# Two mixture-of-experts blocks on one core: weight conversions of the second block spread over both layers, and both entries rearranged

## The chip, the cores and the metric

One core of a Trainium2 chip runs the whole kernel. The metric is the device time of one launch in microseconds (us), the median of the runs shown.

The engines are called as in the profile: PE is TensorE (matmuls; PEld its weight loads), DVE is VectorE, ACT is ScalarE, POOL is GpSimd, SP is SyncE, which here only issues DMAs. Each engine works through its own instructions in order, and waits for others by semaphores.

## The reference

An attention-like layer (8 x 8 heads, 576 rows, no softmax, a decaying causal mask) makes 4608 rows of 512 numbers. Two mixture-of-experts (MoE) blocks with 8 experts follow.

```python
def _moe_ref(x, w_skip, w_gate, w1, w2):          # first block
    do_compute = x @ w_skip > 0
    xc = x[do_compute]
    e_idx = np.argmax(xc @ w_gate, axis=1)
    gate_w = softmax(xc @ w_gate)[chosen]
    for e in range(E):
        h = np.maximum(xc[mask] @ w1[e], 0.0)
        y[mask] = gate_w[mask, None] * (h @ w2[e])
    out[do_compute] = xc + y

def _moe2_ref(x, w_gate, w1, w2):                 # second block
    cap = N // E                                  # 576
    logits = x @ w_gate
    for idx in np.argsort(-logits.flatten()):     # best pair first
        tok, e = idx // E, idx % E
        if assigned[tok] >= 0 or counts[e] >= cap: continue
        assigned[tok] = e; counts[e] += 1
    for e in range(E):
        h = np.maximum(x[mask] @ w1[e], 0.0)      # 512 -> 1024
        out[mask] = h @ w2[e]                     # 1024 -> 512
```

## The kernel before

**Stages.** Attention runs first, up to about 176 us. The first MoE block runs its eight experts (e = 0 to 7) from there to about 480, the second block its eight (i = 0 to 7, in the order in which experts fill up) from there to the end. An expert is a gather of its rows by POOL, a turn of each tile of 128 rows (four transposes on PE, line 641; ACT writes the high half xTH, line 642; DVE the low half xTL, line 179), layer 1 and layer 2.

**Numbers in two halves.** Matmuls of both layers take fp32r operands, and each product is made of three matmuls: high by high, high by low, low by high. So weights too are split: a quarter of w1 or w2 (512 KB) is loaded into one of five `wraw` buffers (`w_load`, line 234), ACT copies it to the high half (`w_split`, line 245: w1H, w2H), and DVE subtracts to get the low half (`w_rest`: w1L, w2L). `halves(kind)` is a list of five jobs that do this for four quarters, the low half of one beside the high half of the next. In the second block, `w2`'s raw quarters stay in their buffers until the tail has read them.

**Layer 1** (`layer1`, `layer1_f`, line 660) goes over eight f of 128 hidden units, in two segments of columns in the second block, (0, 288) and (288, 576), with 12 matmuls each into one of three PSUM buffers. ACT writes hH (line 669), DVE hL (line 188). The last 64 columns go to hT. **Layer 2** has a tail of 64 rows (`layer2_half`, line 714, from hT and raw w2), then four tiles of 128 rows (`layer2`, line 691) with 24 matmuls of 512 columns each. The order of segments and f in a block is such that each w1 quarter serves two consecutive f.

**The first block's hand-written order.** `slot_a()` takes the next of `jobs` between pieces of a layer. The entry (from line 1047) makes three turns with warm-up matmuls between them (`warm`, line 224: 128 columns of ones), and steps the generator `gate_weights()` beside them: an Exp, three parts of gate weights multiplied into MV, and 36 small matmuls `gp` (line 832). In layer 1 of expert 0, the jobs are the loads of the next expert's w1, issued by ACT, and the last gate step. In layer 2, `gate_spread` (line 752) broadcasts the second block's gate weights by SP into the buffers that MV and OHlo leave, for the dot products `gate_dots` (line 758).

**The second block's routing chain.** `phase(i)` finds expert i and its list: five rounds of M (DVE), `cnt` (PE), `part` (DVE), `sum` (PE), `fl` (DVE), `nfl` (PE), `nf` (DVE); then `eix`, the expert's number (DVE); then `pfx`, slots, OHh, MV, OHl (DVE), `idp` and `idq` (PE, lines 1273 and 1282) and `ids2`, the list (DVE); then `cc`, `ccb`, `cct`, and the next phase's Lm, vq, c, mx, OH. `load_b(i)` reads `eix` into a register and makes the loads of this expert's weights.

**The planner.** In the second block PE calls `tick(cols)` within the layers; it advances a clock by cols/2400 and steps each task that is due. A task is a generator that yields the time to its next step; a step is due its yield after the later of its own due time and the clock less 0.4. There are three tasks: the chain of phases, `weights_b(i)` and `rows_b(i)`. In `weights_b(i)`, first the jobs of `halves("w2")` come, 2.3 apart, in layer 1; when expert i+1 is known, its first w1 quarter is loaded; after the tail the three others, then `halves("w1")`, 2.3 apart, then four w2 loads. `rows_b(i)` issues five gathers when the list is there, and five turns, 1.3 apart.

**The second entry** (from line 1372). `late()` runs the last layers of the first block with phase 0; when expert 0 is known, SP loads its two first w1 quarters. When the list is there, five gathers and the conversion of these quarters come, 30 warm-up matmuls, and then turns and steps of the chain (`go`) alternate, with the other loads (two w1 and two w2 quarters by ACT, behind the second turn).

Of the kernel before, what the change touches and what calls it, by code (L numbers as in the profile page):

```python
# [23 lines left out]
P = 128  # L24
# [138 lines left out]
def block_kernel(ctx, tc, q_c, k_c, k_r, v_r, wg, wg2, w1a, w2a, w2t, w1b, w2b, cst, dtab, out, dbg=None):  # L163
# [794 lines left out]
    eix = rt("eix", [P, E], I32)  # L958
    lo0 = rt("lo0", [P, 1])
# [91 lines left out]
    for n, j in enumerate(t0):  # L1051
        next(gws)
        warm(ps1, "l1", 16 if n == 0 else 4)
        j()
    next(gws)
# [34 lines left out]
    for e in range(LATE):  # L1090
        jobs = halves("w2") if e else []
        ga, (la1, la2) = gathers_a(e + 1), loads_a(e + 1)
        if e == 0:
            sta = state()
            jobs += [la1[0], la1[1], lambda: next(gws, None), la1[2], la1[3]]
        else:
            jobs = jobs[0:2] + [ga[0]] + jobs[2:4] + [ga[1]] + jobs[4:5] + [ga[2]] + la1
# [62 lines left out]
    def phase(i):  # L1160
# [124 lines left out]
        ts(iv, p[:, 5:10], -1.0, ALU.add)  # L1285
        stt(ids2[:, i, :], p[:, 0:5], 64.0, iv, ALU.mult, ALU.add)
# [67 lines left out]
    def load_b(i, eng=nc.sync):  # L1354
        r = eng.value_load(eix[0:1, i:i + 1], min_val=0, max_val=E - 1)
        return loads_dyn(r, w1b, w2b, eng=eng)
# [4 lines left out]
    def late():  # L1361
        yield 1.0
        gate_h(1, 0, hh, 7)
        for d in gate_slots(1, L2[:, NT:NC, :]):
            yield d
        for d in last_claims():
            yield d
        for d in phases():
            if not lb and 0 in know:
                lb.extend(load_b(0))  # L1370
                for j in lb[0][0:2]:
                    j()
            yield d

    lb = []
# [5 lines left out]
    while 0 not in listed:  # L1381
        next(gen)
    sp = halves("w1", swap=True)
    for j in gathers_b(0) + sp[0:2]:
        j()
    t0 = turns(("b", 0), T2, (2, 3))
    warm(ps1, "l1", 30)
    go = lambda: next(gen)
    la = load_b(0, nc.scalar)
    for j in [go, go, t0[0], go, t0[1], go] + la[0][2:4] + [t0[2], go, t0[3], la[1][0], la[1][1]] + sp[2:5] + lb[1][2:4]:  # L1390
        j()
# [19 lines left out]

    def weights_b(i):
        for j in halves("w2", swap=True):
            j()
            yield 2.3
# [5 lines left out]
        l1[0]()  # L1421
        while lay[0] < 2 * i + 1 or ("tail", i) not in done:
            yield 0
        for j in l1[1:]:
            j()
        for j in halves("w1", swap=True):
            j()
            yield 2.3
        for j in l2:
            j()  # L1430

    def rows_b(i):
# [7 lines left out]
        yield 3.5  # L1440
        while lay[0] < 2 * i + 1:
            yield 0
        for j in turns(("b", i + 1), T2):
            j()
            yield 1.3

    for i in range(E):
        mine = [task(weights_b(i)), task(rows_b(i))]
        ht = xp.tile([P, 8, 64], F32, name="hT", tag="junk", bufs=1)
        hh = layer1(("b", i), [(0, 288), (288, CAP2)], lambda: None, 1 if i else 2, tick, ht=ht)  # L1450
# [43 lines left out]
```

## Time and profile before

| | us |
|---|---|
| median of 3 runs | 983.54 (982.27 to 983.57) |
| the profiled execution, its own time | 981.48 |
| its span from the first to the last instruction | 979.6 |
| PE busy | 922.7 (94%) |
| DVE busy | 651.1 (66%) |
| ACT busy | 321.9 (33%) |
| POOL busy | 236.1 (24%) |
| mean granted TensorE clock | 0.981 of full |

All stretches and rows are in us from the start of the span of the profiled execution. A row of the timeline gives start, duration, engine, line and operation, the tile written and those read, and in brackets the idle time of its engine before it and what ended it. Durations of PE include the matmul's way through the array, so matmuls in a row overlap; PEclk is the granted clock, 1.00 for 2.4 GHz and 0.50 for 1.2 GHz. The stages can be found by time: first entry 176 to 192, experts of the first block to 480, second entry 480 to 495, blocks 0 to 7 of the second block from 495, 565.5, 626.3, 687.0, 747.6, 808.8, 868.4 and 922.4 on (block 0 lasts to 565.5).

### The profile page before, as it was taken

The page shows a single profiled execution, that of the slowest core. Times are in us where ns is not written, and L with a number is a line of the kernel's source. Part 1 is how long each engine was busy: PE and PEld are TensorE (multiplying, and loading weights), DVE is VectorE, ACT ScalarE, POOL GpSimd, SP SyncE. Part 2 cuts the span into 40 slices and gives each one's busy share as a digit, 9 for nine tenths or more (in the row PEclk, how much of TensorE's full clock was granted, in tenths as well). Part 3 has the DMA queues.
Part 4 walks back from the last instruction along what each step waited for, and adds up shares of the span by engine and source line. Part 5 has one row for each costly group of instructions (what it writes and reads, how often), then busy time and mean ns, then how long its engine had stood idle before and what let it go on. Part 6 is the DMA issues. An engine that isn't in the chain of part 4 may idle for free.

```text
span 979.6 us, 20718 instructions
## 1 busy us (share of the span) xinstructions
PE 922.7 (94%) x8322; PEld 774.5 (79%) x8322; DVE 651.1 (66%) x1676; ACT 321.9 (33%) x610; POOL 236.1 (24%) x208
## 2 busy tenths in 40 slices
PE   8999998599999999998789999999999999999997
PEld 7778876498888888886578697887978869787886
DVE  4566675449999999966686767667676676744230
ACT  1233333133434334351142233332433324333320
POOL 2322231203264334322200303103031030330101
PEclk9999999799999999999979999999999999999999
DMA  9999995355454455330242406125060240732301
GB/s 336 348 372 376 345 358 202 89 206 175 145 206 136 161 178 193 111 133 11 93 166 88 171 12 213 56 74 186 11 234 36 96 163 12 236 103 97 103 6 43
DMA packets 57684, 153.96 MB, mean 157 GB/s; under 512 B 8464, under 2 KB 9232, under 8 KB 57328
## 3 DMA queue, kind: packets, MB, share of 16 engines
q1 hardware_dynamic: 40608, 107.50, 31.4%
q0 software_dynamic: 10496, 30.93, 9.2%
q10 hardware_dynamic: 6480, 14.16, 3.9%
q8 instruction: 67, 1.10, 0.4%
q14 instruction: 33, 0.27, 0.1%
HBM read 127.43 MB, written 25.13 MB: 156 GB/s over the span
## 4 chain that ended last, share of the span: by engine, by line
PE 64%; DVE 23%; DMA 6%; issue 5%; ACT 1%; POOL 0%; SPq 0%; POOLq 0%; ACTq 0%; DVEq 0%
PE l1p L660 27%; PE l2p L691 19%; DVE junk L758 5%; PE l2p L714 3%; DVE w1L L179 3%; PE xTp L445 3%; DVE w2L L179 2%; PE sc L419 2%; DMA X<-xo 2%; DVE xTL L179 2%; PE trp L641 2%; PE xrp L473 1%; PE xTp L442 1%; DMA kT<-in_k_c_dram 1%; DMA qT<-in_q_c_dram 1%
## 5 line engine op out<-in xcount | busy, mean ns | idle before, releaser
L660 PE MATMUL l1p<-xTH,w1H 128*128 128x288 f32 (+1 forms) x768 | 243.2, 317 | 3.6 <-DVE hL L188 2.7
L660 PE MATMUL l1p<-xTL,w1H 128*128 128x288 f32 (+1 forms) x768 | 236.2, 308 | 2.8 <-DVE xTL L179 2.7
L660 PE MATMUL l1p<-xTH,w1L 128*128 128x288 f32 (+1 forms) x768 | 235.3, 306 | 0.0
L691 PE MATMUL l2p<-w2H,hH 128*128 128x512 f32 (+1 forms) x448 | 186.2, 416 | 0.0
L691 PE MATMUL l2p<-w2H,hL 128*128 128x512 f32 (+1 forms) x448 | 176.1, 393 | 0.0
L691 PE MATMUL l2p<-w2L,hH 128*128 128x512 f32 (+1 forms) x448 | 175.3, 391 | 0.0
L660 PEld LDWEIGHTS l1p<-xTH,w1H 128*128 128x128 f32 x768 | 146.5, 191 | 7.9 <-DVE hL L188 5.4
L660 PEld LDWEIGHTS l1p<-xTL,w1H 128*128 128x128 f32 x768 | 146.5, 191 | 3.9 <-DVE xTL L179 3.6
L660 PEld LDWEIGHTS l1p<-xTH,w1L 128*128 128x128 f32 x768 | 146.4, 191 | 0.0
L188 DVE SCALAR_TENSOR_TENSOR hL<-l1p,hH 128x288 fp32r<-128x288 f32 (+1 forms) x192 | 85.7, 453 | 87.2 <-ACT hH L669 85.5
L669 ACT ACTIVATE hH<-l1p 128x288 fp32r<-128x288 f32 (+1 forms) x192 | 78.5, 410 | 179.3 <-PE l1p L660 175.0
L720 POOL DMA_INDIRECT out_dram<-y,ids x40 | 43.3, 1084 | 378.5 <-DVE y L179 218.3
L691 PEld LDWEIGHTS l2p<-w2H,hH 128*128 128x128 f32 (+1 forms) x448 | 82.9, 185 | 23.9 <-issue 8.3
L758 DVE SCALAR_TENSOR_TENSOR junk<-x,wgb 128x512 f32<-128x512 f32 (+1 forms) x144 | 99.0, 688 | 3.1
L691 PEld LDWEIGHTS l2p<-w2H,hL 128*128 128x128 f32 (+1 forms) x448 | 82.6, 184 | 20.7
L691 PEld LDWEIGHTS l2p<-w2L,hH 128*128 128x128 f32 (+1 forms) x448 | 83.1, 185 | 15.0
L621 POOL DMA_INDIRECT xg<-X,ids x64 | 79.3, 1238 | 57.3 <-issue 22.5
L642 ACT ACTIVATE xTH<-trp 128x512 fp32r<-128x512 f32 (+2 forms) x64 | 35.6, 558 | 119.0 <-PE trp L641 91.4
L245 ACT ACTIVATE w1H<-wraw 128x1024 fp32r<-128x1024 f32 x64 | 65.2, 1053 | 25.0 <-DMA wraw<-in_w1b_dram 20.6
L179 DVE TENSOR_TENSOR w1L<-wraw,w1H 128x1024 fp32r<-128x1024 f32 x60 | 71.3, 1219 | 2.5 <-ACT w1H L245 2.0
L245 ACT ACTIVATE w2H<-wraw 128x1024 fp32r<-128x1024 f32 x64 | 67.3, 1054 | 17.2 <-PE l2p L691 7.3
L179 DVE TENSOR_TENSOR w2L<-wraw,w2H 128x1024 fp32r<-128x1024 f32 x60 | 72.7, 1213 | 0.0
(257 smaller groups left out, 1137.5 us busy)
## 6 DMA issues: line engine op xcount, KB each, us to landing
wraw<-in_w2a_dram SPq DMA_DIRECT2D x31, 512.0 KB
wraw<-in_w1b_dram SPq DMA_DIRECT2D x30, 512.0 KB
wraw<-in_w2b_dram SPq DMA_DIRECT2D x30, 512.0 KB
wraw<-in_w1a_dram SPq DMA_DIRECT2D x28, 512.0 KB
kT<-in_k_c_dram SPq DMA_DIRECT2D x36, 256.0 KB
qT<-in_q_c_dram SPq DMA_DIRECT2D x36, 256.0 KB
vR<-in_v_r_dram SPq DMA_DIRECT2D x36, 256.0 KB
X<-xo ACTq DMA_DIRECT2D x36, 256.0 KB
```

The costliest lines, as they stand in the source:

```text
L179: V.tensor_tensor(o, x, y, op)
L188: V.scalar_tensor_tensor(o, x, sc, y, op0, op1)
L245: nc.scalar.activation(h, r, AF.Copy)
L445: nc.tensor.matmul(xTp[o, hh, x:x + P], lhsT=d["vs"][:, 2 * pr + hh, :], rhs=d["ret"][:, hh, pr, :], start=(c == 0), stop=True, skip_group ...
L621: nc.gpsimd.indirect_dma_start(out=t[0:n, :], out_offset=None, in_=X[:, :], in_offset=bass.IndirectOffsetOnAxis(ap=ids[0:n, :], axis=0))
L642: nc.scalar.activation(h[:, :, off:off + n], p[:, :, 0:n], AF.Copy)
L660: nc.tensor.matmul(o, lhsT=wx[:, c:c + P], rhs=xx[:, k, a:b], start=(n == 0), stop=(n == 11))
L669: nc.scalar.activation(hh[0][:, f, a:b], o, AF.Relu)
L691: nc.tensor.matmul(p[0:n, :], lhsT=x[:, f, off:off + n], rhs=y[:, c:c + 512], start=(f == 0 and j == 0), stop=(f == 7 and j == 2))
L714: nc.tensor.matmul(p[64 * h:64 * h + 64, :], lhsT=ht[:, g], rhs=w[g // 2][:, c:c + 512], start=(f == 0), stop=(f == 3), tile_position=(0, ...
L720: nc.gpsimd.indirect_dma_start(out=dst[:, :], out_offset=bass.IndirectOffsetOnAxis(ap=idx, axis=0), in_=src[0:n, :], in_offset=None)
L758: V.scalar_tensor_tensor(j[0:n], x2[0:n], 1.0, wgb[e // 4][0:n, e % 4], ALU.mult, ALU.mult, accum_out=dst[0:n, e:e + 1])
```

## The change

Five things are changed.

1. First entry: the steps of `gate_weights()` no longer stand between the turns. All five go into the jobs of layer 1 of expert 0, alternating with the loads of the next w1; the last one (the matmuls gp) comes after layer 1.
2. Second entry: the loads of the first two w1 quarters come after the list, not when the expert is known, and read the expert's number from a copy `eil`, made just before the list. Their conversions move behind the first steps of the chain, between the turns. There are 64 warm-up matmuls, not 30.
3. Layer 1's segments in the second block are (0, 256) and (256, 576).
4. `weights_b(i)`: of the next expert's w1, quarter 0 is converted in layer 1, quarter 1 in layer 2, quarters 2 and 3 at the beginning of the next layer 1 (`held`), ahead of the w2 quarters. The last w2 load moves there too.
5. `rows_b(i)`: 2.6 instead of 3.5 before the turns, which are 1.8 apart instead of 1.3.

```diff
     t0 = turns(0, T1, (2,))
     for n, j in enumerate(t0):
-        next(gws)
         warm(ps1, "l1", 16 if n == 0 else 4)
         j()
-    next(gws)
     for j in gathers_a(1):
         j()
...
-            jobs += [la1[0], la1[1], lambda: next(gws, None), la1[2], la1[3]]
+            jobs += [j for n in range(4) for j in (lambda: next(gws, None), la1[n])] + [lambda: next(gws, None)]
...
         ts(iv, p[:, 5:10], -1.0, ALU.add)
+        if i == 0:
+            V.tensor_copy(eil, eix[:, 0:1])
         stt(ids2[:, i, :], p[:, 0:5], 64.0, iv, ALU.mult, ALU.add)
...
     def load_b(i, eng=nc.sync):
-        r = eng.value_load(eix[0:1, i:i + 1], min_val=0, max_val=E - 1)
+        r = eng.value_load(eix[0:1, i:i + 1] if i else eil[0:1, 0:1], min_val=0, max_val=E - 1)
...
         for d in phases():
-            if not lb and 0 in know:
-                lb.extend(load_b(0))
-                for j in lb[0][0:2]:
-                    j()
             yield d
...
+    lb = load_b(0)
     sp = halves("w1", swap=True)
-    for j in gathers_b(0) + sp[0:2]:
+    for j in lb[0][0:2] + gathers_b(0):
         j()
     t0 = turns(("b", 0), T2, (2, 3))
-    warm(ps1, "l1", 30)
+    warm(ps1, "l1", 64)
     go = lambda: next(gen)
     la = load_b(0, nc.scalar)
-    for j in [go, go, t0[0], go, t0[1], go] + la[0][2:4] + [t0[2], go, t0[3], la[1][0], la[1][1]] + sp[2:5] + lb[1][2:4]:
+    for j in [go, go, sp[0], t0[0], sp[1], go, t0[1], go] + la[0][2:4] + [t0[2], go, t0[3], la[1][0], la[1][1]] + sp[2:5] + lb[1][2:4]:
         j()
...
     def weights_b(i):
+        if held:
+            for c in (2, 3):
+                w_split("w1", c, "later", swap=True)
+                yield 1.2
+                w_rest("w1", c)
+                if c == 2:
+                    held.pop()()
+                yield 1.2
         for j in halves("w2", swap=True):
             j()
             yield 2.3
...
         l1, l2 = load_b(i + 1)
         l1[0]()
+        yield 3.0
+        w_split("w1", 0, "later", swap=True)
+        yield 1.5
+        w_rest("w1", 0)
         while lay[0] < 2 * i + 1 or ("tail", i) not in done:
             yield 0
         for j in l1[1:]:
             j()
-        for j in halves("w1", swap=True):
+        yield 2.3
+        w_split("w1", 1, "later", swap=True)
+        yield 2.3
+        w_rest("w1", 1)
+        for j in l2[0:3]:
             j()
-            yield 2.3
-        for j in l2:
-            j()
+        held.append(l2[3])
...
-        yield 3.5
+        yield 2.6
...
         for j in turns(("b", i + 1), T2):
             j()
-            yield 1.3
+            yield 1.8
...
-        hh = layer1(("b", i), [(0, 288), (288, CAP2)], lambda: None, 1 if i else 2, tick, ht=ht)
+        hh = layer1(("b", i), [(0, 256), (256, CAP2)], lambda: None, 1 if i else 2, tick, ht=ht)
```

## Rows read from the trace of the kernel before

**Rows 1.** Page, busy us of each engine, share of the span, instructions.

```profile
PE 922.7 (94%) x8322; PEld 774.5 (79%) x8322; DVE 651.1 (66%) x1676; ACT 321.9 (33%) x610; POOL 236.1 (24%) x208
```

**Rows 2.** Stretches: us; busy PE, PEld, DVE, ACT, POOL; PEclk, DMA share, GB/s.

```profile
534.03:565.53 31.50, 29.25 (x174) 21.81 (x175) 20.03 (x60) 9.19 (x13) 10.29 (x9) 0.95 0.51 180
565.53:593.26 27.73, 27.73 (x242) 26.84 (x243) 19.09 (x62) 11.00 (x27) 1.31 (x1) 1.00 0.08 30
...
596.84:626.30 29.46, 27.60 (x175) 20.91 (x175) 19.64 (x58) 9.08 (x13) 10.17 (x9) 1.00 0.55 192
...
778.94:808.75 29.81, 27.59 (x176) 20.94 (x175) 19.55 (x58) 9.08 (x13) 10.00 (x9) 1.00 0.53 190
840.06:868.36 28.30, 27.58 (x174) 21.34 (x174) 18.42 (x62) 9.07 (x13) 10.49 (x9) 1.00 0.64 220
```

**Rows 3.** PE's waits, 500 to 880: us in total, times, longest.

```profile
PE trp L641 <- DVE xTL L179: 6.8, 10, 2.0
```

**Rows 4.** PE in order of time: start, us, what, [idle before <- releaser].

```profile
552.08 0.65 PE L641 MATMUL trp<-cs,xg 128*128 128x128 f32 x4 [2.04 <-DVE xTL L179]
...
597.58 0.87 PE L1273 MATMUL idp<-MV,OHl 128*128 128x160 bf16 x10
...
612.94 0.66 PE L641 MATMUL trp<-cs,xg 128*128 128x128 f32 x4 [1.30 <-DVE xTL L179]
```

**Rows 5.** DVE in order of time, block 1, end of layer 1 and layer 2.

```profile
592.35 0.45 DVE L188 SCALAR_TENSOR_TENSOR hL<-l1p,hH 128x288 fp32r<-128x288 f32 x1
...
595.14 0.89 DVE L179 TENSOR_TENSOR OHl<-hl,kq 128x640 bf16<-128x640 bf16 x2
...
602.64 2.36 DVE L179 TENSOR_TENSOR w1L<-wraw,w1H 128x1024 fp32r<-128x1024 f32 x2
...
612.20 0.68 DVE L179 TENSOR_TENSOR xTL<-trp,xTH 128x512 fp32r<-128x512 f32 x1
```

**Rows 6.** ACT in order of time, end of block 1's layer 1.

```profile
591.70 0.41 ACT L669 ACTIVATE hH<-l1p 128x288 fp32r<-128x288 f32 x1 [1.28 <-PE l1p L660]
```

**Rows 7.** SP's queue, block 1, and DMA in a stretch (columns as rows 2).

```profile
588.51 8.69 SPq L234 DMA_DIRECT2D wraw<-in_w1b_dram  x4
...
591.25:591.50 0.25, 0.25 (x5) 0.25 (x4) 0.21 (x2) 0.00 (x0) 0.00 (x0) 1.00 0.01 0
```

**Rows 8.** First entry: PE, then DVE, then ACT, in order of time.

```profile
189.55 0.43 PE L660 MATMUL l1p<-xTH,w1H 128*128 128x352 f32 x1 [0.82 <-ACT xTH L642]
192.33 0.66 PE L660 MATMUL l1p<-xTL,w1H 128*128 128x352 f32 x1 [2.35 <-DVE xTL L179]
...
191.72 0.55 DVE L179 TENSOR_TENSOR xTL<-trp,xTH 128x384 fp32r<-128x384 f32 x1
...
189.01 0.49 ACT L642 ACTIVATE xTH<-trp 128x384 fp32r<-128x384 f32 x1 [0.20 <-PE trp L641]
```

**Rows 9.** Stretches at half clock, columns as rows 2.

```profile
191.20:194.70 3.50, 2.37 (x8) 2.38 (x9) 1.88 (x6) 0.00 (x0) 0.00 (x0) 0.51 0.21 83
194.70:198.10 3.40, 3.40 (x14) 3.40 (x13) 0.53 (x1) 0.46 (x1) 0.00 (x0) 0.50 0.28 98
553.20:556.60 3.40, 3.40 (x20) 2.73 (x20) 1.43 (x4) 0.54 (x2) 0.00 (x0) 0.51 0.10 36
```

**Rows 10.** Second entry: SP, ACT, POOL, the chain, PE, in order of time.

```profile
476.12 1.01 SPq L234 DMA_DIRECT2D wraw<-in_w1b_dram  x2
...
479.28 1.06 ACT L245 ACTIVATE w1H<-wraw 128x1024 fp32r<-128x1024 f32 x1 [10.85 <-DMA wraw<-in_w1b_dram]
...
483.16 0.92 POOL L720 DMA_INDIRECT X<-x,ids  x1 [5.23 <-DVE pt L1276]
486.70 1.01 POOL L621 DMA_INDIRECT xg<-X,ids  x1 [2.62 <-DVE X L179]
...
493.59 5.79 DMA wraw<-in_w1b_dram
...
504.03 0.41 PE L1192 MATMUL cnt<-OH,M 128*128 128x32 bf16 x10 [0.96 <-DVE M L179]
```

More of the change, by code (lines that the diff above doesn't have):

```diff
@@ L958, in block_kernel @@
     eix = rt("eix", [P, E], I32)
+    eil = rt("eil", [P, 1], I32)
     lo0 = rt("lo0", [P, 1])
@@ L1368, in late @@
         for d in phases():
-            if not lb and 0 in know:
-                lb.extend(load_b(0))
-                for j in lb[0][0:2]:
-                    j()
             yield d
-    lb = []
     gen = late()
@@ L1410, in block_kernel @@
     done = set()
+    held = []
     def weights_b(i):
+        if held:
[6 more added lines that the diff above has]
+                yield 1.2
         for j in halves("w2", swap=True):
```

## The prediction

> **What bounds the kernel now.** I read the page's engine shares first: TensorE (PE) is busy for 94% of the span [rows 1]. What a change can win is therefore the time in which PE waits or runs at half clock, at about 57 us in all. Next came the busy times by stretch. A block of the second MoE is layer 1, a half-tile tail and layer 2. In layer 1 (565.53 to 593.26) PE is busy for all of 27.73 us; in layer 2 it is busy for 27.6 us, but the stretch lasts 29.46 in block 1, the same within 0.1 in blocks 2 and 3, 29.81 in block 4, 28.30 in block 5 and 31.50 in block 0 [rows 2]. So each of these blocks leaves 0.7 to 2.3 us idle, all in layer 2. The waits say who: transposes (line 641) wait for xTL, 6.8 us in ten waits, the longest 2.0 [rows 3, 4]. VectorE (DVE) explains why: from 602.64 on it takes four w1L subtractions of 1.18 us amid the routing steps, and the first xTL ran only at 612.20 [rows 5]. The PSUM buffer came free late, and the third turn waited 1.30 us [rows 4]. Of the two entries I read PE and what ends its waits. At the first, the second matmul waits 2.35 us for the last xTL [rows 8], and the clock then falls [rows 9]. At the second, the chain runs through gathers and weight loads [rows 10].
>
> **The change, part by part.**
>
> *First entry.* The four gate-weight steps leave the stretch before layer 1. Two of them stood between the three xTL on DVE. Without them the last xTL needs only its xTH, which ends at 189.01 + 0.49 = 189.50 [rows 8]; with about 0.5 for the subtraction, PE goes on at 190.03 instead of 192.33: **2.3 us**. The steps (DVE work and one Exp) run under the first layer, where DVE has only one hL per f; without that cover they would cost the 2.3 us again. The 36 gp matmuls stay one run on PE, now after layer 1; no change. Queues they pass: ScalarE's (ACT) loads for expert 1 go out one to four slots later, still before layer 1 ends, and are converted in layer 2; SP's two gate-weight broadcasts wait for gp, so they move from the middle of layer 1 to its end, ahead of SP's w2 loads, and are first read after layer 2's first tile. I take 0 for both, and 1 us as the bad end.
> The clock: PE was at half speed from 191.2 to 198.1 (mean 0.51, then 0.50) [rows 9], with 2.37 + 3.40 = 5.77 us busy; at full speed this is half, **2.9 us** less. Does it still fall? In layer 2 a wait of 1.30 us did not lower the clock (block 1, 29.46 less 27.60 is all idle), one of 2.04 did [rows 2, 4, 9]. What is left here is the 0.82 before 189.55 [rows 8], nearer to the first: I take 2.9, with 0 as the other end. Entry one: **5.2**, ends 1.3 and 5.2.
> Ahead of 189.55 PE has transposes, with only a few warm-up matmuls between them. If these do not hold the clock, it falls as before, which is rival 1. The Trainium skill ("TensorE: Matmul & The Clock Gate", Part 4) has this as a rule: a transpose does not count as PE activity in the way that a matmul does. By that rule entry one would give 2.3 and not 5.2; the rows of before do not show which.
>
> *Second entry.* The two first w1 loads leave 476.12 [rows 10] for the time after the list. Gain: the scatter before the last ran beside them, so the last one left only at 483.16, after 5.23 us idle on GpSimd (POOL), and the first gather, which reads what it wrote, stood 2.62 us idle behind it, until 486.70 [rows 10]. Without the loads that gather starts up to 2.6 us earlier; I take 1.6, near 485.1. Loss: the loads now run beside the gathers, and w1H of the first quarter, which ACT takes in order, stands ahead of the first xTH, the second ahead of the second xTH. A load beside one scatter was taken up 479.28 - 476.12 = 3.16 us after its issue [rows 10]; issued after the list, near 485.3, the quarters land near 489 and, beside the gathers, 491, so the second xTH ends near 493. Only then does ACT issue the last two w1 quarters, at 493.59 before. The chain goes on from there as it did: 5.79 us of load [rows 10], w1H, w1L, the last xTL, OH, M, and the counting matmuls, on which PE waits at 504.03 [rows 10]. The 256-column first segment (two turns) and the 64 warm-up matmuls help PE before that point only, and PE waits there anyway. I take **0**, with -2 (load and gather slow each other as the scatter was) and +2 (all of the gather's lead) as ends; the copy into eil is inside these.
>
> *Segments.* Columns per f stay 576. No matmul of 256 columns with fp32r operands is in the trace: if each took as long as one of 288, the 96 of a block would lose a ninth of at most 27.73/192 = 0.144 each, 1.5 us a block and 12 in all. Ten matmuls of 160 columns take 0.87 [rows 4], 0.087 each, so I see no floor there and take 0.
>
> *Blocks.* I worked out the planner's clock (each tick adds columns/2400; a step is due its yield after the later of its due time and the clock less 0.4). Layer 1 is 23.04, the tail 3.41, layer 2 20.48, and the routing chain keeps its place, one list per block at 28.37. In blocks 1 to 5, w1 quarters 2 and 3 go to 0.6 to 4.2, the w2 quarters from 0.7-10.1 to 5.8-15.0, quarter 0 of the next expert to 20.8 and 22.2, quarter 1 stays in layer 2; the turns run from 34.1 in steps of 1.9. Layer 1's DVE goes from 19.09 to about 22.5 of 27.73 us, ACT's from 11.0 to 14.2 [rows 2]: no PE wait from load alone, since one subtraction (1.18) in front of a routing step is what w2L already does there without a wait.
> The last w2 quarter, loaded only when quarter 2 of w1 is done (2.1), is converted at 12.8, ten us later; SP has nothing queued behind it.
> In layer 2 one of three early w1L remains and the two around the turns go: the first xTL moves up from 612.2 by about 3 us, and the waits of [rows 3] go: 1.86 in block 1, 1.76 and 1.78 in 2 and 3, 2.2 in 4, 0.7 in 5.
> **What is late next** is the early quarter. Its load is issued at 588.51, when the expert is known; its packets end by 591.25 [rows 7], so it can be taken up at about 592.0. ACT comes to it before that and is held; after 1.06 of w1H the hH due at 591.70 [rows 6] starts at 593.1, hL behind it on DVE at 593.5 instead of 592.35, and the work from there to the end of OHl, 3.7 us almost without a gap [rows 5], plus the new w1L of 1.18, ends at 598.3. PE wants OHl at 597.6 to 597.7 [rows 4]: a new wait of **0.6 us** in each of blocks 1 to 5. So they give 1.26, 1.16, 1.18, 1.61 and 0.10: 5.3. In block 0 the expert is known at 19.20 of the planner's clock, not 17.28: two us later, so the wait is 2.6, over the 2.04 that lowered the clock, and that cost 29.25 busy us against 27.60, 1.65 more [rows 2]. Block 0: 27.6 + 2.6 + 1.65 = 31.85, **-0.3**. Blocks: **5.0**. Ends: 0 (the load 0.8 later) and 12.2 (no new wait).
>
> *Sum.* 5.2 + 0 + 5.0 = 10.2. The profiled execution took 981.48, 1.9 more than its span; it becomes 971.3. The median of the runs, 983.54, is 2.06 above it: **973.3 us**.
>
> **Rivals.**
> 1. *The clock falls at the first entry all the same*, because what stands ahead of 189.55 is mostly transposes. The gain is 2.3 there, 7.3 in all: 976.2. For it: the clock fell there before; against it: the wait of 2.35 that went with that is gone [rows 8, 9].
> 2. *The waits only change place.* The new wait at the list's matmuls eats what the turns give back (blocks: 0), loads and gathers hinder each other (-2), and the clock falls (2.3): 983.2, no change. For it: DVE is packed in that stretch [rows 5].
> 3. *Slower: the early load holds ACT past the end of layer 1.* If it is taken up 1.5 us later than I put it, the list's matmuls wait 2.1 us in blocks 1 to 5 and 4.1 in block 0, and each such wait lowers the clock as the 2.04 did: 27.6 + 2.1 + 1.65 = 31.35 against 29.4, five times 1.9, and 33.35 against 31.5: 11.3 lost, less 5.2: 989.6. It decides at a wait between 1.30 and 2.04 us, that is, a load 0.7 to 1.4 later. Against it: nothing else loads then; the 512 KB ran alone. For it: other ACT work is behind it in order.
> 4. *The load lands before ACT asks*: no new wait, 12.2 + 5.2: 966.1.
>
> **How the numbers follow.** Forecast 0.58 (its own range 968 to 979, by the ends of entry two and of the blocks together); rival 1 0.14, rival 2 0.13, rival 3 with the 256-column floor 0.12, rival 4 0.03. Faster by over 0.2% (2 us, about what can be told from no change): 0.58 + 0.14 + 0.03 = 0.75; within: 0.13; slower: 0.12. The range 967 to 982 leaves out rival 4, rival 3 and the upper half of rival 2, a little under 0.2.
>
> **What would show it.** Right: PE's second layer-1 matmul right after the first at the first entry, with no half clock until layer 1 ends; no wait of transposes for xTL in blocks 0 to 5; a wait of about 0.6 before idp (2.6 in block 0), with DVE's hL held by ACT; the second entry's M at the same distance from the list. Wrong: waits before counting matmuls in layer 1, w1H waiting for its load over 2 us, a PEclk under 1.0 in layer 2 of blocks 1 to 5, or layer 1 longer than 27.8 us.

## The result, and the profile after

| | us |
|---|---|
| before, median of 8 runs beside it | 983.18 (979.95 to 988.38) |
| after, median of 8 runs | 972.08 (969.09 to 978.59) |
| ratio, 95% interval | 0.9904 (0.9874 to 0.9934) |
| after, the profiled execution and its span | 971.05 and 969.3 |

The ratio is estimated from all runs; it is not the quotient of the two medians, which would be 0.9887. Forecast were 973.3 for the median and 971.3 for the profiled execution. Both sums came out nearly right, but two of the terms were wrong by 4 to 5 us, in opposite directions. So the profile comes first, in the order of the prediction.

The busy row of the page, after:

```profile
PE 918.6 (95%) x8356; PEld 768.9 (79%) x8356; DVE 653.6 (67%) x1677; ACT 320.2 (33%) x610; POOL 232.6 (24%) x208
```

PE does the same work in a shorter span [rows 1]. Now the stretches that answer [rows 2] (columns as there): layer 2 of block 0, layer 1 and layer 2 of block 1.

```profile
533.54:562.72 29.18, 27.66 (x175) 20.73 (x174) 19.43 (x62) 6.11 (x10) 8.89 (x9) 1.00 0.48 177
562.86:590.38 27.52, 27.52 (x240) 26.55 (x239) 20.70 (x59) 13.79 (x30) 1.30 (x1) 1.00 0.13 49
594.00:621.56 27.56, 27.56 (x176) 20.91 (x175) 17.41 (x59) 6.11 (x10) 10.21 (x9) 1.00 0.53 187
```

Layer 2 of block 1 has no idle time left (27.56 of 27.56, against 27.60 of 29.46), and layer 1 carries the moved work without a wait, with DVE at 20.7 of 27.5 us. Block 0 keeps 1.5 us idle, but its clock no longer falls (1.00, against 0.95). PE's waits from 500 to 880, the answer to [rows 3]:

```profile
PE idp L1272 <- DVE OHl L179: 1.8, 3, 0.9
PE l1p L660 <- DVE xTL L179: 1.4, 1, 1.4
PE cnt L1191 <- DVE M L179: 0.9, 1, 0.9
PE trp L641 <- DMA xg<-X,ids: 0.4, 1, 0.4
```

The ten waits of transposes for xTL are gone. The new wait before idp that I expected in every block is there in blocks 0 and 3 only. The first entry, answering [rows 8 and 9]: PE in order of time, then two stretches.

```profile
190.39 0.42 PE L660 MATMUL l1p<-xTH,w1H 128*128 128x352 f32 x1 [0.58 <-ACT xTH L642]
190.98 0.43 PE L660 MATMUL l1p<-xTL,w1H 128*128 128x352 f32 x1 [0.17 <-DVE xTL L179]
```

```profile
190.39:194.00 3.61, 3.44 (x20) 3.20 (x21) 1.36 (x3) 0.91 (x2) 0.00 (x0) 1.00 0.04 15
194.00:198.00 4.00, 4.00 (x27) 4.00 (x26) 2.46 (x9) 0.93 (x2) 0.00 (x0) 1.00 0.43 140
```

The 2.35 us wait has become 0.17, and the clock stays full. From the first layer-1 matmul to the first of layer 2 it took 22.01 us before (189.55 to 211.56) and takes 17.11 now (190.39 to 207.50).

Where the 10.4 us between the two profiled executions lie, worked out from such boundaries of PE in both traces (plus is gained): attention's end -0.7; first entry with the first expert's layer 1 +4.8; the rest of the first block's experts **-2.6**; second entry, up to the tail of block 0, -1.0; tail and layer 2 of block 0 +2.2; blocks 1 to 5 +2.1, +2.1, +1.7, +2.0, +0.7; blocks 6 and 7 **-0.4 and -0.5**. Nothing that I costed can lengthen the three stretches in bold. The last chain pieces show where the two at the end come from: in each kernel, the 192 layer-1 matmuls and the last 72 layer-2 matmuls of the last block, as the chain has them (start, us, what). Before, then after:

```profile
922.38 25.43 PE l1p L660 x192
951.39 16.58 PE l2p L691 x72
```

```profile
911.60 25.28 PE l1p L660 x192
940.46 17.01 PE l2p L691 x72
```

No wait and no lower clock is in them: the same 72 matmuls take 0.43 us longer. The same in the group of layer-2 matmuls of the first block (line 691, high half of h by low half of w2; busy us, mean ns of one), before, then after:

```profile
L691 PE MATMUL l2p<-w2L,hH 128*128 128x512 f32 x384 | 150.3, 391 | 0.0
```

```profile
L691 PE MATMUL l2p<-w2L,hH 128*128 128x512 f32 x384 | 151.6, 395 | 0.0
```

So three questions were put to the chip: did the clock at the first entry hold because the wait is gone; what in the blocks' part won, and why did the new wait stay away; and what slowed layer 2.

### The profile page after: what moved, and what is told of

It is laid out like the page before. It is cut to its first block, busy times and chain, and to the rows that moved or that the text cites. A ratio compares the mean times of both kernels' runs of the same rounds, so it can differ in the third digit from the quotient of the medians.

```text
span 969.3 us, 20752 instructions
## 1 busy us (share of the span) xinstructions
PE 918.6 (95%) x8356; PEld 768.9 (79%) x8356; DVE 653.6 (67%) x1677; ACT 320.2 (33%) x610; POOL 232.6 (24%) x208
## 4 chain that ended last, share of the span: by engine, by line
PE 72%; DVE 15%; DMA 7%; issue 3%; ACT 1%; SPq 1%; POOL 1%; POOLq 0%; ACTq 0%; DVEq 0%
PE l1p L660 27%; PE l2p L691 26%; DVE junk L758 5%; PE xTp L445 3%; PE trp L641 3%; PE l2p L714 2%; PE sc L419 2%; DVE w2L L179 2%; DMA vR<-in_v_r_dram 2%; DMA xg<-X,ids 2%; PE xrp L473 1%; DVE xTL L179 1%; DMA kT<-in_k_c_dram 1%; DVE hL L188 1%; PE xTp L442 1%
## 5 line engine op out<-in xcount | busy, mean ns | idle before, releaser
L660 PE MATMUL l1p<-xTH,w1H 128*128 128x320 f32 (+2 forms) x768 | 241.4, 314 | 4.9 <-DVE hL L188 3.0
L660 PE MATMUL l1p<-xTL,w1H 128*128 128x320 f32 (+2 forms) x768 | 234.2, 305 | 2.9 <-DVE xTL L179 2.9
L660 PE MATMUL l1p<-xTH,w1L 128*128 128x320 f32 (+2 forms) x768 | 233.7, 304 | 0.0
L188 DVE SCALAR_TENSOR_TENSOR hL<-l1p,hH 128x256 fp32r<-128x256 f32 (+1 forms) x192 | 85.6, 453 | 80.6 <-ACT hH L669 77.1
L669 ACT ACTIVATE hH<-l1p 128x256 fp32r<-128x256 f32 (+1 forms) x192 | 78.3, 408 | 147.7 <-PE l1p L660 141.1
```

Of the source, the lines that this page charges most:

```text
L188: V.scalar_tensor_tensor(o, x, sc, y, op0, op1)
L660: nc.tensor.matmul(o, lhsT=wx[:, c:c + P], rhs=xx[:, k, a:b], start=(n == 0), stop=(n == 11))
L669: nc.scalar.activation(hh[0][:, f, a:b], o, AF.Relu)
```

## The experiments

Each kernel ran beside the kernel before on one chip. The ratios:

| kernel | median us | before beside it | ratio to before, 95% interval |
|---|---|---|---|
| first entry alone (e1_gate) | 979.04 | 982.20 | 0.9961 (0.9939 to 0.9984) |
| blocks alone (e2_blocks) | 972.93 | 982.20 | 0.9906 (0.9875 to 0.9938) |
| second entry alone (e3_entry) | 988.39 | 982.20 | 1.0050 (1.0031 to 1.0070) |
| segments alone (e4_segs) | 985.50 | 982.20 | 1.0017 (0.9995 to 1.0039) |
| unused 4-byte tile (g1_pad32) | 986.79 | 981.93 | 1.0048 (1.0027 to 1.0068) |
| unused 64-byte tile (g2_pad64) | 984.72 | 981.93 | 1.0036 (1.0014 to 1.0057) |
| changed, tiles put back (g3_aligned) | 970.83 | 981.93 | 0.9899 (0.9864 to 0.9933) |
| the same with 288 and 288 (g4_best) | 970.66 | 981.93 | 0.9887 (0.9853 to 0.9922) |
| changed, no warm-up (f3_nowarm) | 971.73 | 983.38 | 0.9881 (0.9848 to 0.9913) |
| changed, early load late (h1_late) | 979.13 | 983.38 | 0.9957 (0.9932 to 0.9983) |
| turns alone (h2_turns) | 984.40 | 983.38 | 1.0005 (0.9986 to 1.0025) |
| conversions alone (h3_weights) | 973.25 | 983.38 | 0.9896 (0.9872 to 0.9920) |

### The four parts, one at a time

**First entry alone**: part 1 of the change, the rest as before.

> The kernel before with the first entry's part alone: the gate-weight steps moved into the first expert's layer 1. Theory (the clock fell because of the wait of 2.35 us for the last xTL): that wait goes, the second layer-1 matmul follows the first within 0.2 us, and no slice is at half clock before layer 1 ends; 4.7 us less than the kernel before, near 978.5. Rival (what stands ahead of layer 1 is mostly transposes, so the clock falls all the same): a half-clock stretch of some 7 us from 191, and 2.3 us less, near 980.9. Layer 2 of the first MoE: 0.235 us from one 512-column matmul to the next, as before, if the slower pace of the changed kernel (0.239) comes from its extra tile eil; anything between if it varies by itself.

Measured: 3.8 us less by the ratio (1.6 to 6.0). PE at the entry, and a stretch:

```profile
190.15 0.43 PE L660 MATMUL l1p<-xTL,w1H 128*128 128x352 f32 x1 [0.17 <-DVE xTL L179]
```

```profile
189.56:193.00 3.44, 3.27 (x19) 3.04 (x20) 1.17 (x3) 0.91 (x2) 0.00 (x0) 1.00 0.02 6
```

Its trace has what the changed kernel has: 17.21 us from the first layer-1 matmul to layer 2 (189.56 to 206.77), the clock at 1.00. The blocks' kernel is the counterpart, since it has the entry of before: a wait, then half clock. PE, then three stretches:

```profile
190.15 0.66 PE L660 MATMUL l1p<-xTL,w1H 128*128 128x352 f32 x1 [2.11 <-DVE xTL L179]
```

```profile
187.61:190.15 2.54, 0.43 (x2) 0.19 (x2) 2.51 (x8) 0.00 (x0) 0.00 (x0) 0.99 0.56 216
190.15:193.50 3.35, 3.35 (x11) 3.35 (x12) 0.74 (x3) 0.00 (x0) 0.00 (x0) 0.50 0.02 5
193.50:197.00 3.50, 3.50 (x51) 3.37 (x51) 1.16 (x3) 0.93 (x2) 0.00 (x0) 1.00 0.45 150
```

Both have the same transposes and warm-up matmuls ahead; with the wait the clock falls, without it not. All the traces at hand say the same wherever the clock was up as layer 1 began: in the seven with the entry of before, waits of 1.92 to 2.89 us were followed by half clock; in the five with the new entry and its warm-up matmuls the wait is 0.16 to 0.31 us and the clock stays. But it was down for 3.4 us here, not for the 6.9 of [rows 9], and cost 1.7 us, not 2.9. Layer 1 of the first expert took 22.0 to 22.3 us in four of the eight traces with the old entry, 20.5 to 21.1 in the other four, and 17.1 to 17.4 in those five with the new one. So the kernel before was profiled in one of the longer executions, which may be why this part is worth somewhat less over many runs.

**Blocks alone**: `weights_b`, `rows_b` and `held` as in the changed kernel, the rest as before.

> The kernel before with the blocks' part alone (early first quarter, quarters 2 and 3 held over to the next layer 1, turns from 2.6 in steps of 1.8). By the prediction's working, 5.0 us less: 978.2, with a wait of 0.6 us before the list's matmuls in blocks 1 to 5 and of 2.6 in block 0. By what the changed kernel's trace shows (no such wait in blocks 1, 2, 4 and 5), 10.7 less: 972.5, and no transposes that wait for xTL in blocks 0 to 5.

Measured: 9.2 us less (6.1 to 12.3). In its trace block 0 is 2.2 us shorter and blocks 1 to 5 together 7.4. So the reading of the trace is confirmed, and the prediction's 5.0 is too small by nearly half. PE waits for idp three times, 2.1 us in all, and never for xTL in a turn.

**Second entry alone**: `load_b`, `late`, the copy into eil, the order of the entry, 64 warm-up matmuls.

> The kernel before with the second entry's part alone (first two w1 loads after the list, the copy into eil, the longer warm-up). The prediction took 0: 983.2. Theory from the changed kernel's trace: 1 us longer, 984.2, since the quarters' w1H then stand on ScalarE in the middle of the turns. If the tile eil, which moves every later SBUF address by a few bytes, is what slows the layer-2 matmuls from 0.235 to 0.239 us in the first MoE, 4 to 5 us come on top: 988.5.

Measured: 4.9 us slower by the ratio (3.0 to 6.9), a median of 988.4, which of the three theories only that of the tile's place gave. The entry itself costs nothing: from the end of the first block's layers to the tail of block 0 it took 50.01 us, against 50.05 before. Over all traces at hand this stretch has a mean of 50.25 us with the old entry (eight kernels, 48.97 to 51.32) and of 50.31 with the new one (six, 49.68 to 51.05). The 1.0 us lost there in the first comparison is this scatter.

**Segments alone**: part 3 of the change, the rest as before.

> The kernel before with the segments alone (256 and 320 columns in place of 288 and 288). The prediction took 0: 983.2. Rival: 256-column matmuls take as long as 288-column ones, 1.5 us a block, 12 in all: 995. By the changed kernel's trace (0.117 us from one 256-column matmul to the next, 0.147 for 320, 0.132 for 288 before) the sum of a pair is the same, so 983.2 and layer 1 of a block at 27.7 us.

Measured: 1.7 us slower, which cannot be told from no change, and no floor. In the trace, layer 1 of a block is 27.91 us for 27.80 in blocks 1 to 5 and 25.69 for 25.52 in blocks 6 and 7: about 1 us in all.

### What slowed layer 2

All tiles behind `eix` in the same memory move when a tile is added. In the kernel before, hL, hH, xTH and xTL start at bytes 162944, 181376, 208000 and 217216 of each partition, all multiples of 128. `eil` holds 4 bytes but takes 32, so in the changed kernel all four start 32 bytes further; the weights w1 and w2 lie ahead of it and stay. Two kernels add an unused tile and nothing else:

```diff
     eix = rt("eix", [P, E], I32)
+    eil = rt("eil", [P, 1], I32)
...
+    V.memset(eil, 0)
```

> The kernel before with an unused tile of 4 bytes a partition beside eix (it takes 32 bytes and moves xg, hL, hH, xTH and xTL from multiples of 128 bytes to 32 bytes beyond one); no other edit but its memset. Theory (the position in SBUF sets the pace of the matmuls): layer 1 of a full block 27.93 us in place of 27.80, tail and layer 2 of the last block 26.25 in place of 25.66, the first MoE's layer-2 matmuls (w2L) 395 to 396 ns in place of 391; 5 to 6.5 us more, near 988. Rival (the copy into eil, its wait or the later loads slow the second entry's kernel): no change, 982.2.

> As the one with the 4-byte tile, but the tile has 64 bytes, so that hL, hH, xTH and xTL start 64 bytes beyond a multiple of 128. If a multiple of 64 is enough, 982.2 and the old durations (w2L 391 ns, last block's tail and layer 2 25.66). If it must be one of 128, near 988 as with 32. If the position does not matter at all, both are at 982.2.

Measured: 4.7 us slower with the 4-byte tile (2.7 to 6.7), 3.5 with the 64-byte tile (1.4 to 5.6). The last chain pieces, 4-byte tile, then 64-byte tile:

```profile
926.57 25.60 PE l1p L660 x192
955.76 17.00 PE l2p L691 x72
```

```profile
956.00 17.00 PE l2p L691 x72
```

A tile that nobody reads gives the 17.00 of the changed kernel, and a mean of 396 ns for the group that had 391. So it is not the copy, its wait or the later loads. Layer 2, whose loaded weights are hH and hL, minds both positions; they are the only operands of these matmuls that moved. Layer 1 with segments of 288, which streams xTH and xTL, minds 32 bytes (25.60 for 25.43) but hardly 64 (its 192 took 25.47). Worked out from the timelines, layer 2 goes from one matmul to the next in 228 to 230 ns where hH and hL lie on multiples of 128 and in 232 to 234 where they do not, but only with tiles of 128 rows: the first block's tiles of 96 rows take 229 to 231 either way (the first matmul of each three left out). For layer 2 a multiple of 128 is good and one of 64 alone is not; other positions were not tried, and why PE is slower is not shown.

The counter-test gives the 32 bytes back, by putting two one-column tiles into one:

```diff
-    lo0 = rt("lo0", [P, 1])
-    top = rt("top", [P, 1])
+    lt0 = rt("lo0", [P, 2])
+    lo0, top = lt0[:, 0:1], lt0[:, 1:2]
```

> The changed kernel with lo0 and top in one tile, so that eil's 32 bytes are given back and hL, hH, xTH and xTL lie where they lay in the kernel before. Theory: tail and layer 2 of the blocks lose 0.5 us each and the first MoE 1 us, 5.0 in all; layer 1 with 256 and 320 columns goes to 27.91 from 27.66, 1.7 back: 3.3 less than the changed kernel, near 969.5. Rival (position has nothing to do with it): as the changed kernel, 972.8.

Its last chain pieces and its group of layer-2 matmuls:

```profile
911.24 25.59 PE l1p L660 x192
940.42 16.58 PE l2p L691 x72
```

```profile
L691 PE MATMUL l2p<-w2L,hH 128*128 128x512 f32 x384 | 150.1, 391 | 0.0
```

Layer 2 is back at 16.58 and 391 ns. The total is not what I expected: 0.9899 against 0.9904, about 0.5 us where 3.3 were expected, and the intervals do not tell them apart. Layer 1 with 256 and 320 columns is the slower one here, 25.59, where 32 bytes further it had been the fastest of all, 25.28; from one matmul to the next those of 256 columns take 119.5 ns here and 117 there, those of 320 columns 147 in both. That loss was in the expectation. New waits were not. PE's waits from 500 to 880, those of transposes and idp:

```profile
PE trp L641 <- DMA xg<-X,ids: 1.8, 4, 0.8
PE idp L1272 <- DVE OHl L179: 1.6, 2, 1.0
```

Turns wait 1.8 us for gathers where the changed kernel had 0.4: presumably because a faster layer 2 brings them up sooner; that was not followed further.

With the old segments on top (part 3 of the change undone):

> The changed kernel with lo0 and top in one tile and the segments of the kernel before (288 and 288). Theory: layer 1 at 27.80 and 25.52 in place of 27.91 and 25.69, 1.0 us less than with 256 and 320: near 968.5. Rival (the second entry needs the short first segment): the second entry 1 us longer, 969.5 to 970.5.

Measured: 0.9887, the chain's layer 1 and layer 2 as before the change, and again 1.8 us of waits for gathers. It is 1.7 us under the changed kernel by the ratios; the two intervals overlap for the most part, so this is not shown to be better. The first entry and the blocks alone had won 3.8 and 9.2; this kernel, which has both and the second entry, wins 11.1 (7.7 to 14.4), so whether the parts simply add up stays open.

### What in the blocks' part wins

**Turns alone**: 2.6 and 1.8 in place of 3.5 and 1.3.

> The kernel before with the turns alone respaced (2.6, then steps of 1.8, in place of 3.5 and 1.3); the four w1 subtractions stay in layer 2. Theory (these subtractions are what makes xTL late): the waits of transposes for xTL stay, 1 to 2 us a block; 980 to 983 in all. Rival (the spacing is the whole of it): the waits go and the time is that of the blocks' part, 972.9.

Measured: 1.0005, nothing won. The time agrees with the theory, the mechanism with neither: the waits for xTL do go, and another takes their place. PE's waits for M from 500 to 880, before, then here; and DVE from block 1's layer 2:

```profile
PE cnt L1192 <- DVE M L179: 4.2, 5, 1.0
```

```profile
PE cnt L1192 <- DVE M L179: 10.2, 6, 2.7
```

```profile
613.75 1.22 DVE L179 TENSOR_TENSOR w1L<-wraw,w1H 128x1024 fp32r<-128x1024 f32 x1
614.88 0.68 DVE L179 TENSOR_TENSOR xTL<-trp,xTH 128x512 fp32r<-128x512 f32 x1
615.82 0.83 DVE L179 TENSOR_TENSOR M<-zb,kq 128x1280 bf16<-128x1280 bf16 x1
```

DVE takes the subtraction and the turn first, M comes behind both, and the counting matmuls wait 10.2 us for M, where before the transposes had waited 6.8 for xTL and the counting matmuls 4.2 for M. The queue was too full; its order only chose the victim. With the waits of 1.70, 1.95 and 2.66 in blocks 0, 2 and 4 the clock fell to 0.50 for 3.4 us; with that of 2.30 in block 3 it stayed at 1.00.

**Conversions alone**: `weights_b` and `held` as in the changed kernel, the turns as before.

> The kernel before with the w1 conversions alone spread (quarter 0 early, quarters 2 and 3 in the next layer 1); the turns keep 3.5 and steps of 1.3. Theory: without the subtractions around them the turns are on time whatever their spacing, and nearly all of the blocks' gain is here: 973 to 975. Rival: turns 1.3 apart still wait for one another's xTL and buffer, half of the gain: 977.

Measured: 0.9896, as much as both together. In its trace blocks 1 to 5 take 58.4 to 58.9 us each, more evenly than with the new turns (58.8 to 59.5 in the blocks' kernel), and PE's waits name no transposes; the longest in all is:

```profile
PE idp L1273 <- DVE OHl L179: 2.0, 3, 1.1
```

The two w1 subtractions that left layer 2 for the next layer 1, and the early one, are the whole of it as far as these runs can tell. Turns that start at 2.6 come to their rows before the gathers have landed (0.8 us of waits in the blocks' kernel), those at 3.5 do not. Both new entries and the conversions, with the old turns, the old segments and the tiles put back, are the combination that this points to; it was not run.

### How much slack the early quarter has

The third rival said that a load only 0.7 to 1.4 us later turns the change into a loss. Here the loads read the expert's number from a copy that DVE makes behind the steps that follow it (in one of the two places where this is done, cut):

```diff
             ts(eix[:, i:i + 1], mc, -1.0, ALU.mult, 8.0, ALU.add)
-            yield "expert"
...
             stt(sb[:, 0], asg, mc, ge, ALU.is_equal, ALU.add)
+            V.tensor_copy(eil[:, i:i + 1], eix[:, i:i + 1])
+            yield "expert"
...
-        r = eng.value_load(eix[0:1, i:i + 1] if i else eil[0:1, 0:1], min_val=0, max_val=E - 1)
+        r = eng.value_load(eil[0:1, i:i + 1], min_val=0, max_val=E - 1)
```

> The changed kernel with the expert's number copied once more, behind the two steps that follow it on VectorE, and the loads reading the copy: in blocks 1 to 5 the early quarter's load goes out some 1.6 us later, everything else in place. By the third rival's rule (a load 0.7 to 1.4 us later than forecast makes waits that lower the clock): w1H starts 1.6 us later, hL and the one-hots behind it too, the list's matmuls wait about 1.5 us a block, and if the clock falls as well 1.65 more each: 972.8 + 5 x 1.4 + 1.5 = 981 with the clock up, near 990 with it down. If there is more slack than that: 972.8.

Measured: 0.9957, some 5 us of the gain gone. In block 1, w1H starts 27.42 us after layer 1's start, 1.1 later than in the changed kernel. Block 0's idp in its two halves, then block 1's w1H and idp; and three stretches (columns as [rows 2]), two from block 0 and the tail and layer 2 of block 1.

```profile
536.80 0.52 PE L1274 MATMUL idp<-MV,OHl 128*128 128x160 bf16 x5 [1.60 <-DVE OHl L179]
537.92 0.70 PE L1274 MATMUL idp<-MV,OHl 128*128 128x160 bf16 x5 [0.60 <-DVE OHl L179]
...
592.24 1.06 ACT L245 ACTIVATE w1H<-wraw 128x1024 fp32r<-128x1024 f32 x1 [2.48 <-DMA wraw<-in_w1b_dram]
...
597.95 0.92 PE L1274 MATMUL idp<-MV,OHl 128*128 128x160 bf16 x10 [0.92 <-DVE OHl L179]
```

```profile
538.00:539.50 1.50, 1.50 (x8) 1.31 (x9) 0.32 (x1) 0.00 (x0) 0.67 (x1) 0.54 1.00 385
539.50:543.00 3.50, 3.50 (x28) 2.36 (x27) 1.25 (x9) 0.00 (x0) 0.27 (x1) 0.71 0.27 105
592.60:624.90 32.30, 31.11 (x188) 21.71 (x188) 21.04 (x67) 7.48 (x14) 10.28 (x9) 1.00 0.48 164
```

The chain from the early quarter to idp is as the rival has it: 1.1 us later makes a wait of 0.92. Blocks 1 to 5 lose 1.0 to 1.4 us each against the changed kernel, at full clock. In block 0, waits of 1.60 and 0.60 one behind the other did lower it (0.54, then 0.71 in the slices), and that block lost 2.7. So the rival's chain is real, but 1.1 us later the change still wins 4.2 us (1.7 to 6.6): the price that it put on each wait, a lowered clock, was paid in block 0 alone.

### Whether warm-up matmuls hold the clock

```diff
     for n, j in enumerate(t0):
-        warm(ps1, "l1", 16 if n == 0 else 4)
         j()
```

> The changed kernel without the 24 warm-up matmuls ahead of and between the three turns of the first entry, so that only transposes stand between the end of the attention and layer 1. Theory (a wait of over 2 us on PE is what lowered the clock): the granted clock stays at 1.0 through layer 1, whose matmuls follow at 0.16 us; as the changed kernel, 972, or up to 2.5 us less, since 1.89 and 0.63 us of warm-up go. Rival (transposes do not keep the clock up): a stretch at half clock at the start of layer 1, matmuls 0.29 us apart, some 2.9 us lost there, which about eats what the warm-ups took: 972 to 975.

PE at the first entry without them, then two stretches:

```profile
186.76 2.61 PE L641 MATMUL trp<-cs,xg 128*128 128x128 f32 x12 [8.19 <-issue]
189.95 0.66 PE L660 MATMUL l1p<-xTH,w1H 128*128 128x352 f32 x1 [0.58 <-ACT xTH L642]
```

```profile
186.70:189.90 3.20, 2.61 (x12) 2.31 (x12) 1.20 (x2) 1.69 (x3) 2.23 (x3) 0.50 0.28 83
189.95:193.40 3.45, 3.45 (x10) 3.08 (x11) 0.97 (x3) 0.44 (x1) 0.55 (x1) 0.50 0.46 134
```

My theory here was wrong: PE stood at half clock through the transposes and went on at half clock for the first 3.4 us of layer 1 and about one more, with no wait over 0.58 us. But the clock did not fall there. It was down when the first transpose began, behind 8.19 us in which PE was idle. The changed kernel has such a pause too, before its warm-up matmuls; and in the kernel with the 64-byte tile, which has all 24 of them, layer 1 began at half clock. The changed kernel, then the one with the 64-byte tile:

```profile
184.97 1.89 PE L224 MATMUL idle<-ones 128*128 128x128 bf16 x16 [7.88 <-issue]
```

```profile
189.00:189.70 0.70, 0.70 (x8) 0.62 (x6) 0.11 (x2) 0.60 (x1) 0.00 (x0) 0.71 0.54 205
```

```profile
191.47 0.66 PE L660 MATMUL l1p<-xTH,w1H 128*128 128x352 f32 x1 [0.58 <-ACT xTH L642]
```

In the changed kernel the clock is at 0.50 from 184.97 and comes up in the stretch shown, 1.0 us before layer 1. So the warm-up matmuls do not hold a clock that is up: with them it mostly comes up before layer 1, and without them it came up behind its start. Whether that is because transposes do less for it or because PE had less work behind the pause, these runs do not separate. From the first layer-1 matmul to layer 2 it took 18.92 us without them, not 17.11. The total is the same all the same (0.9881 against 0.9904), since layer 1 began 1.9 us earlier, counted from the last matmul ahead of the pause (11.38 against 13.30 us): the 24 warm-up matmuls cost about what the clock gives.

## Why the prediction came out right, and which of its terms were wrong

**First entry: right in its sum, with luck in the clock.** The step that counted, the last xTL needing only its xTH, holds to 0.1 us or so: the wait is 0.17. The clock did stay up, and 4.9 us came of it in the two profiled executions (5.2 forecast), 3.8 in the part alone by all its runs. The 2.9 us for the clock were read from one execution whose half-clock stretch was a long one. Rival 1 fell, but not for the reason that I gave. I took the size of the last wait as what decides. What I did not look at is that the clock was already down when the entry began, behind 7.9 us in which PE was idle, and that it has to come up before layer 1: it did so by 1.0 us in the changed kernel, and did not in two others, one of them without warm-up matmuls. I had called these "only a few"; without them layer 1 of the first expert takes 18.92 us and not 17.11. That layer 1 begins at half clock without them is what the rule of the Trainium skill ("TensorE: Matmul & The Clock Gate", Part 4) would give, by which transposes do not count as PE activity in the way of a matmul. But that kernel also gives PE less work behind the pause, so it does not single the rule out.

**Second entry: right at 0**, with a lead and a loss of the kind that I had put down. Counted from the list (ids2), the first gather starts 1.4 us behind it and not 2.8; but beside the loads the first transposes start 5.9 us behind that gather and not 3.4. The ends of -2 and +2 are wider than the scatter of that stretch, 2.4 us. But "the copy into eil is inside these" is the sentence that was wrong. The copy costs nothing; the place that its tile takes costs 4.7 us (2.7 to 6.7) on the kernel before. Worked out from the traces of the 4-byte tile: 0.13 us in layer 1 of each of blocks 1 to 5 and 0.17 in the last two, 0.5 to 0.6 in each of the last two layers 2 with their tails, and 1.1 in the first block's experts; in the layers 2 of blocks 0 to 5, where PE of the kernel before waits anyway, hardly 0.2 in all. That is some 3.4 of the 4.7.

The first block's experts took 271.4 to 271.6 us in five of the six kernels with the 32 or 64 bytes, and 270.4 to 270.5 in six of the eight without. The other three, the kernel before (268.8), turns alone (268.9) and the late load (270.1), are 1.4 to 1.7 us shorter than their like, and their traces show why. Near the end of these experts PE waits 0.64 to 0.68 us and then 1.68 or 1.69 before counting matmuls, in all fourteen kernels. In these three the clock stays at 1.00; in the eleven others it goes to 0.50 for 3.4 us at the end of the second wait or just behind it. The second wait and that stretch in the changed kernel, then the stretch at the same wait (455.55) in the kernel before:

```profile
452.62 0.18 PE L1191 MATMUL cnt<-OH,M 128*128 128x32 bf16 x1 [1.69 <-DVE OH L179]
```

```profile
452.23:455.64 3.41, 3.02 (x12) 1.58 (x12) 0.64 (x4) 0.00 (x0) 0.65 (x1) 0.50 0.20 77
```

```profile
455.20:458.60 3.40, 3.05 (x18) 1.97 (x18) 1.71 (x7) 0.00 (x0) 0.62 (x1) 1.00 0.20 77
```

So of the 2.6 us lost there between the two profiled executions 1.1 are eil's place and the rest is the clock, which goes with no part of the change. Why the same waits lower it in one execution and not in another is not shown. It also means that the size of a wait alone does not decide, as I had it with "between 1.30 and 2.04 us": the wait of 1.69 came with a lower clock in eleven executions and not in three, and one of 2.30 with the turns alone did not lower it.

**Segments: right at 0 to within 1 us.** The wider surprise is that the sign depends on the position: 256 and 320 columns take 0.17 us more than 288 and 288 in the last block where the tiles lie on multiples of 128, and 0.3 less (25.28 against 25.60) where they lie 32 bytes on. In the changed kernel this gave back some 2 us of what eil took: 0.27 us in each layer 1.

**Blocks: the mechanism right, the price wrong.** The waits for xTL went, as forecast, and layer 1 took the work. (The idle time that I put down to them was not theirs alone: in blocks 2 to 4 about 1.0 us each was counting matmuls that waited for M, and that went with them.) The failing step is "what is late next". Its chain is nearly as I put it; counted from the end of layer 1, forecast and measured: w1H taken up 1.3 us ahead of it in both; the next hL 0.2 behind it and 0.0; OHl done 5.0 and 4.7 behind. The rows of block 1, after:

```profile
589.06 1.06 ACT L245 ACTIVATE w1H<-wraw 128x1024 fp32r<-128x1024 f32 x1 [1.39 <-DMA wraw<-in_w1b_dram]
590.42 0.42 DVE L188 SCALAR_TENSOR_TENSOR hL<-l1p,hH 128x256 fp32r<-128x256 f32 x1 [0.72 <-ACT hH L669]
594.23 0.88 DVE L179 TENSOR_TENSOR OHl<-hl,kq 128x640 bf16<-128x640 bf16 x2
594.77 0.92 PE L1272 MATMUL idp<-MV,OHl 128*128 128x160 bf16 x10
```

But idp starts at 594.77, while OHl's second half still runs: each of its first five matmuls needs the first half only, ready 0.4 us earlier. I compared PE's start with the end of the whole one-hot. Block 0 of the late-load kernel above shows the halves apart, five matmuls behind each. The two errors, 0.3 and 0.4 us, are more than the 0.6. In block 0 the waits were 0.92 and 0.60 and not 2.6, by the same halves and because idp stands three matmuls, 0.7 us, later in that block; the clock did not fall there, and the term was +2.2 and not -0.3. By the part alone the blocks gave 9.2 (6.1 to 12.3), between my 5.0 and the 12.2 of no new wait.

**The sum.** Forecast 5.2 + 0 + 5.0. By the parts alone: 3.8 + 9.2, less 4.7 for eil's place, less 1.7 for segments alone, plus some 3 that the segments and that place give together: 9.6, against 9.4 by the ratio of the whole. Each of these parts has an interval of some 2 to 3 us to either side, so the sum is a sketch. But that the total agrees is two missed terms, one of each sign, and so in part luck. Rival 2 had one of its waits right in another kernel: respaced turns alone do only move the wait. Rival 3 did not come about even with the load 1.1 us later, which took 5 of the 9 us and not all; rival 4, with 0.03, came nearest to what the blocks did.

Of the signs that I named: no half clock, no wait for xTL, the list's wait in two blocks only, and the second entry at the same distance within its scatter. Of the signs against none came that was new: w1H's wait of 1.99 us in block 0 was the nearest, and the 0.9 us before counting matmuls in block 0's layer 1 had been there before, as 0.96 [rows 10]. But none could have shown the pace of the matmuls themselves: "layer 2 has no idle" looks the same at 391 and at 395 ns, and only counting like with like, in a block that nothing touches, shows it.

## What to carry to other kernels

A new tile, however small, moves all that is allocated behind it: after such an edit, compare the duration of matmuls in a stretch that the edit should not touch, and give the bytes back if they changed. When an engine's queue is too full, taking work out of the stretch wins and reordering it only picks who waits; and a wait that you forecast has to be compared with the part of the operand that the first instruction reads, not with the whole tile.

## What the runs showed of the hardware

- The start of the tiles that PE reads sets its pace by 1 to 2.5%: hH and hL 32 or 64 bytes off a multiple of 128 make 72 layer-2 matmuls take 17.00 us for 16.58, with tiles of 128 rows and not with those of 96; xTH and xTL 32 bytes off make 192 layer-1 matmuls of 288 columns take 25.60 for 25.43, but with 256 and 320 columns 25.28 for 25.59. The Trainium skill ("SBUF — State Buffer", Operand start alignment) has the start of an operand as a matter of what is allowed, not of speed; these runs add a speed.
- The clock falls with waits of about 2 us, and not always. At one of 1.68 or 1.69 us, with one of 0.64 to 0.68 two us ahead of it, PE went to the lower of its two levels, 1.2 GHz, in eleven of fourteen executions, for 3.4 us each time. Waits of 1.60 and 0.60 in a row lowered it too, 0.92 and 0.60 and a single 2.30 did not. With a wait of 2.11 us it was down for 3.4 us, with one of 2.35 for 6.9.
- After 7.9 and 8.2 us of idle time PE began at 1.2 GHz. With twelve transposes alone behind that pause it was still there when layer 1 began; with 24 small matmuls ahead of and between them it was at 2.4 GHz by then, but for one execution of thirteen.
